# Fused block-sparse attention and ELU MLP: three of eight half-batches turned by VectorE and a DRAM scratch

## The chip, the cores and the metric

One core of a Trainium2 chip runs the whole program. The metric is device microseconds for one execution, the median of several. The core has TensorE (PE in the profile: matmuls; PEld: its weight loads), VectorE (DVE), ScalarE (ACT), GpSimd (POOL) and SyncE (SP). Each runs its own list of instructions in order, and waits on semaphores for the others. In this program SyncE does nothing but issue transfers, for 16 DMA engines.

## What is computed

Attention of 4 batches x 8 heads over 768 tokens with 64 dimensions. Each query takes, of the 24 chunks of 32 keys, the 6 with the largest upper bound of its scores. Then a two-layer MLP with ELU over the heads side by side:

```python
k_min, k_max = k_chunks.min(axis=3), k_chunks.max(axis=3)
ub = sum(maximum(q * k_min, q * k_max))           # per query and chunk, causal
sel = the 6 chunks with the largest ub
scores = where(sel & (i >= j), (q @ k.T) / 8, -1e9)
attn = softmax(scores) @ v                        # [4, 8, 768, 64]
x = attn.transpose(0, 2, 1, 3).reshape(3072, 512)
h = x @ w_in                                      # [3072, 2048]
g = where(h > 0, h, exp(min(h, 0)) - 1)
out = g @ w_out                                   # [3072, 512], float32
```

## The kernel before

Heads go in pairs, so that 2 x 64 dimensions fill the 128 partitions: pairs 0 to 3 are batch 0, pairs 4 to 7 batch 1, and so on. Queries go in halves of 384 (`HALF`), `hf` 0 or 1. For a pair and half, `pair_attend` makes the scores (L863) in pieces, takes their exponential on ScalarE (L890), and multiplies by v with a column of ones (L922, called PV below). VectorE takes the reciprocal of the row sums (L935) and multiplies (L938): the tile `on` holds 128 queries x 3 query tiles x 128 features. The MLP needs x with features on the partitions, so TensorE turns `on` in three 128x128 transposes into a PSUM bank (L947), and ScalarE copies the bank to SBUF as half of the tile `xT` (L950).

`mlp(b, hf)` multiplies by w_in in 16 blocks of 128 features of the hidden layer (L972, "up", four matmuls to a block, one for each pair), applies ELU with ScalarE (L982, L987) and VectorE (L990 to L1016), and multiplies by w_out (L1032, "down", in quarters of four matmuls), for three tiles of 128 tokens. ScalarE copies each tile to a result buffer `osb` (L1041), of which there are three, and SyncE stores it (L1046).

The order of work isn't left to a scheduler. The function is traced into a list of operations, each with its engine, what it reads and writes, and which buffers it takes and frees. `QUEUE` holds, for each engine, the numbers of these operations in the order in which the engine runs them; `Plan.order` only merges the five lists and hands out the numbered buffers, with a model of durations and of the DMA rings (`ALONE`, `SHARE`, `PAUSE`, `RAMP`). So PE's list mixes the MLP of one batch with the attention of the next. The number of buffers of each kind stands in `caps`:

```python
caps = {"S2": 2, "ps": 4, "H": 3, "O": 2, "T": 2, "M": 2, "MT": 2, ...,
        "pt": 10, "t": 3, "gT": 3, "osb": 3, "on": 3, "rc": 3, "xT": 8}
```

A buffer is taken again only when all that used it is over, a transfer out of it included. Loads of q, k and v and stores of results all stand in SyncE's one list; the eight weight transfers are issued by GpSimd. Keys and queries of batches 1 to 3 are loaded in pieces of 128 bytes (L592) and turned by VectorE in 32x32 blocks (L604, L622).

Of the kernel before, what the change touches and what calls it, by code (L numbers as in the profile page):

```python
# [14 lines left out]
BF16 = mybir.dt.bfloat16  # L15
# [58 lines left out]
    ],  # L74
    "POOL": [
# [10 lines left out]
    ],  # L86
    "ACT": [
# [20 lines left out]
    ],  # L108
# [5 lines left out]
    ],  # L114
# [43 lines left out]
class Plan:  # L158
# [71 lines left out]
    SHARE = {128: 1.0, 256: 0.35, 512: 0.3, 768: 0.3, 1024: 0.3, 2048: 0.5}  # L230
    HEAVY = 0.088
    RAMP = 240.0
    PAUSE = ((0.0, 2.28), (17.2, 17.8), (21.6, 22.4), (30.5, 31.3))
    LANDED = 0.75

    def served(self, rings, t, until):
# [877 lines left out]
```

## Time and profile before

| | |
|---|---|
| median of 3 runs | 273.88 us (272.23 to 274.41) |
| the profiled execution | 273.46 us, of which 271.8 us from its first to its last instruction |
| granted TensorE clock | 0.998 |
| packets moved by DMA | 112624, 29.79 MB; 101200 of them under 512 bytes |
| chain of work that ended last, PE's share | 78% |

A view of groups names the source line, the engine, the operation, what is written and read, and the count; then the busy time, the mean time of one, and the idle time of the engine just before, with what ended it. A view in order of time gives the start, the length, and in brackets the idle time before a row. In a view of stretches each engine has its busy time in that stretch, and then come the granted clock (1 is full), the mean busy share of the 16 DMA engines, and GB/s.

### The profile page before, as it was taken

To read this page: it belongs to the slowest core of one execution; us is meant where nothing else is said; L and a number is where in the kernel's file an instruction comes from. 1 tells how busy PE (TensorE), PEld (TensorE's weight loads), DVE (VectorE), ACT (ScalarE), POOL (GpSimd) and SP (SyncE) were. 2 spreads that over 40 slices of the span, in tenths; PEclk is the share of its full clock that TensorE was granted. 3 is DMA by queue.
4 is the path that set the end of the run, shared out by engine and by line. 5 is a ranking of instruction groups with operands and counts; after the bars stand their busy time and mean duration, and the time that the engine had idled before them with its cause. 6 is when DMAs were issued, how large, how long until landed. Compare 5 with 4: busy or idle time off the path is not lost.

```text
span 271.8 us, 6603 instructions
## 1 busy us (share of the span) xinstructions
PE 258.6 (95%) x2456; PEld 160.0 (59%) x2456; DVE 206.8 (76%) x532; ACT 200.0 (74%) x375; POOL 118.3 (44%) x209
## 2 busy tenths in 40 slices
PE   3898899999999899999999999999999999999995
PEld 3787566655565455655565556665666655555544
DVE  5698979899999979889998867786666875137530
ACT  3899999846996589989899478977898744243512
POOL 3577783155876696870874055544330000000000
PEclk9999999999999999999999999999999999999999
DMA  7997999999999995999931010000210101110113
GB/s 218 266 211 124 205 216 214 164 176 151 148 203 130 192 169 115 139 156 201 240 103 41 1 58 22 0 2 3 76 41 1 41 2 39 39 41 0 65 53 116
DMA packets 112624, 29.79 MB, mean 110 GB/s; under 512 B 101200, under 2 KB 109648, under 8 KB 112592
## 3 DMA queue, kind: packets, MB, share of 16 engines
q1 hardware_dynamic: 107280, 24.39, 48.5%
q0 software_dynamic: 4224, 4.19, 9.3%
q10 hardware_dynamic: 1088, 0.79, 0.9%
q8 instruction: 19, 0.31, 0.5%
q14 instruction: 13, 0.11, 0.1%
HBM read 27.26 MB, written 6.29 MB: 123 GB/s over the span
## 4 chain that ended last, share of the span: by engine, by line
PE 78%; ACT 7%; DVE 6%; DMA 6%; issue 1%; SPq 1%; POOL 0%; DVEq 0%; ACTq 0%; POOLq 0%
PE psH L972 20%; PE psM L1032 20%; PE psS L863 10%; PE psS L972 8%; PE psMT L1032 8%; PE psO L922 6%; ACT pt L890 3%; DMA w_in_sb<-in_moe_w_in_dram 3%; PE psS L771 2%; ACT lhs L695 2%; PE psT L947 2%; DMA out_dram<-osb 1%; PE psMT L685 1%; DMA gT<-in_k_dram 1%; PE psH L685 1%
## 5 line engine op out<-in xcount | busy, mean ns | idle before, releaser
L890 ACT ACTIVATE pt<-psS 128x768 bf16<-128x768 f32 (+1 forms) x120 | 89.8, 781 | 11.3 <-PE psS L863 6.7
L972 PE MATMUL psH<-xT,w_in_sb 128*128 128x384 bf16 x384 | 73.7, 326 | 0.5 <-DMA w_in_sb<-in_moe_w_in_dram 0.4
L1032 PE MATMUL psM<-w_out_sb,gT 128*128 128x512 bf16 x288 | 72.1, 379 | 0.0
L972 PEld LDWEIGHTS <-w_in_sb 128*128 128x128 bf16 x512 | 47.7, 97 | 33.1 <-issue 1.3
L863 PE MATMUL psS<-rhs,lhs 88*128 88x384 bf16 (+4 forms) x304 | 54.6, 283 | 2.8 <-ACT pt L890 2.8
L1032 PEld LDWEIGHTS <-gT 128*128 128x128 bf16 x400 | 37.3, 97 | 33.0 <-DVE gT L1016 0.5
L982 ACT ACTIVATE f<-psH 128x384 f32<-128x384 f32 x96 | 47.0, 506 | 7.0 <-PE psH L972 6.1
L909 POOL TENSOR_SCALAR_AFFINE_SELECT pt<-pt 128x512 bf16<-128x512 bf16 (+1 forms) x48 | 24.7, 522 | 61.6 <-ACT pt L890 58.1
L1011 DVE SCALAR_TENSOR_TENSOR t<-f,psH 128x384 bf16<-128x384 f32 x56 | 30.1, 547 | 12.9 <-ACT f L982 12.4
L863 PEld LDWEIGHTS <-lhs 88*128 88x128 bf16 x304 | 27.4, 98 | 17.8 <-issue 3.0
L737 POOL CAST rhs<-f 64x768 bf16<-64x768 f32 (+1 forms) x40 | 27.7, 698 | 20.4 <-DVE f L622 8.6
L821 POOL COPY rhs<-selt 24x576 bf16<-24x576 bf16 (+2 forms) x40 | 22.7, 566 | 24.2 <-DVE selt L810 22.5
L922 PEld LDWEIGHTS <-pt 128*128 128x128 bf16 x672 | 28.3, 98 | 7.4 <-issue 1.0
L1016 DVE SCALAR_TENSOR_TENSOR gT<-psH,t 128x384 bf16<-128x384 f32 x56 | 30.5, 551 | 1.1
L922 PE MATMUL psO<-vext,pt 128*128 128x65 bf16 x672 | 31.1, 194 | 0.1
L950 ACT ACTIVATE xT<-psT 128x384 bf16<-128x384 bf16 x32 | 15.6, 497 | 11.9 <-PE psT L947 11.9
L972 PE MATMUL psS<-xT,w_in_sb 128*128 128x384 bf16 x128 | 22.9, 326 | 0.0
L982 ACT ACTIVATE f<-psS 128x768 f32<-128x768 f32 x16 | 13.0, 811 | 13.5 <-PE psS L972 13.5
L990 DVE SCALAR_TENSOR_TENSOR gT<-f,psH 128x384 bf16<-128x384 f32 x40 | 21.3, 541 | 2.0 <-ACT psH L987 1.3
L1032 PE MATMUL psMT<-w_out_sb,gT 128*128 128x512 bf16 (+1 forms) x112 | 22.6, 349 | 0.0
L737 POOL CAST lhs<-f 64x768 bf16<-64x768 f32 x24 | 19.7, 823 | 6.4 <-DVE f L604 5.5
L987 ACT ACTIVATE psH<-psH 128x384 f32<-128x384 f32 x40 | 20.2, 512 | 0.0
(55 smaller groups left out, 278.9 us busy)
## 6 DMA issues: line engine op xcount, KB each, us to landing
out_dram<-osb SPq DMA_DIRECT2D x23, 256.0 KB, 2.2
f<-in_k_dram SPq DMA_DIRECT2D x48, 96.0 KB, 3.9
f<-in_q_dram SPq DMA_DIRECT2D x48, 96.0 KB, 3.8
f<-in_v_dram SPq DMA_DIRECT2D x24, 192.0 KB, 3.9
w_in_sb<-in_moe_w_in_dram POOLq DMA_DIRECT2D x4, 512.0 KB, 9.2
w_out_sb<-in_moe_w_out_dram POOLq DMA_DIRECT2D x4, 512.0 KB, 14.7
gT<-in_k_dram SPq DMA_DIRECT2D x8, 192.0 KB, 4.3
gT<-in_v_dram SPq DMA_DIRECT2D x12, 128.0 KB, 4.2
```

The source lines that it names most:

```text
L737: nc.gpsimd.tensor_copy(out=o, in_=i)
L821: eng.tensor_copy(out=dst.rearrange("c h (i two x) -> c h i two x", two=2, x=32)[:, :, :, odd, :], in_=tiles[st][r0:r0 + NCH, c0:c0 + n].r ...
L863: nc.tensor.matmul(p_s[:, hd, pc:pc + w], lhsT=tiles[pt_["kb"]][0:64 + NCH, hd, 128 * kb:128 * kb + 128], rhs=tiles[pt_["qb"]][0:64 + NCH, ...
L890: lambda bs=bs, pt=pt, wtot=wtot, lo=lo, at=at: nc.scalar.activation(out=tiles[pt][:, :, lo:lo + wtot], in_=tiles[bs[0]][:, :, at:at + wto ...
L909: nc.gpsimd.affine_select(out=a, in_=a, compare_op=AOT.is_ge, fill=0.0, base=0, pattern=pat, channel_multiplier=-1)
L922: nc.tensor.matmul(po[:, hd, qi, :], lhsT=tiles[pt][:, hd, off:off + 128], rhs=tiles[pt_["vx"]][:, 6 * hd + kb, :], start=(kb == 0), stop= ...
L972: nc.tensor.matmul(ph, lhsT=w_in_sb[:, kk, f0:f0 + 128], rhs=tiles[XT[4 * b + kk]][:, c0:c0 + HALF], start=(kk == 0), stop=(kk == NKK - 1))
L982: lambda e=e, view=view: nc.scalar.activation(out=halves(e)[:, 0:step], in_=view(), func=AF.Exp),
L990: lambda e=e, view=view, fc=fc, gt=gt: nc.vector.scalar_tensor_tensor(out=tiles[gt][:, fc:fc + step, :], in0=halves(e)[:, 0:step], scalar= ...
L1011: lambda e=e, t=t, view=view: nc.vector.scalar_tensor_tensor(out=tiles[t][:, 0:step], in0=halves(e)[:, 0:step], scalar=1.0, in1=view(), op ...
L1016: lambda t=t, view=view, fc=fc, gt=gt: nc.vector.scalar_tensor_tensor(out=tiles[gt][:, fc:fc + step, :], in0=view(), scalar=0.0, in1=tiles ...
L1032: nc.tensor.matmul(pm, lhsT=tiles[gt][:, fc, 128 * tt:128 * tt + 128], rhs=w_out_sb[:, fc, x0:x1], start=(fc == 0), stop=(fc == NFC - 1))
```

## The change

For the halves in `TURN`, both of batch 2 and the first of batch 3, `on` no longer goes to TensorE. VectorE transposes its 32x32 blocks into a second tile of the same kind, `xb`; four transfers write that to a scratch in DRAM so that the blocks land where the whole transpose has them, in pieces of 96 elements; and one transfer loads the scratch as half of `xT`. The columns of `xT` are then in another order of tokens: column 96i + 32t + r of the half holds its token 128t + 32i + r. So the stores of these halves go out in two parts each, to the rows to which they belong. The other halves are done as before. In `pair_attend`:

```diff
+            if (u // 4, hf) in TURN:
+                xb, = new("on")
+                there = dram.tile([P, HALF], BF16, name=f"xd{u}_{hf}")
+                def flat(h):
+                    return tiles[h].rearrange("p q h d -> p (q h d)")
+                def blocks():
+                    nc.vector.transpose(out=flat(xb).rearrange("p (j t x) -> p t j x", j=4, x=32),
+                                        in_=flat(on).rearrange("p (t j x) -> p t j x", j=4, x=32))
+                def put():
+                    for i in range(4):
+                        nc.sync.dma_start(out=there[:, 96 * i:96 * i + 96].rearrange("(j a) y -> a j y", j=4),
+                                          in_=flat(xb)[32 * i:32 * i + 32].rearrange("a (j y) -> a j y", j=4))
+                add("DVE", dve(HALF), pr, blocks, reads=[on], writes=[xb], alloc=[xb], free=[on])
+                fetch(4, 128, 192, pr, put, [("put", u, hf)], more=[xb], free=[xb])
+                fetch(1, 128, 768, pr,
+                      lambda: nc.sync.dma_start(out=tiles[xt_h][:, HALF * hf:HALF * hf + HALF], in_=there[:, :]),
+                      [(xt_h, hf)], more=[("put", u, hf)], alloc=[] if hf else [xt_h])
+                return
             bx = bank("T")
```

And in `mlp`, where a tile of results is stored:

```diff
+                    if (b, hf) in TURN:
+                        def put(osb=osb, row=b * S + HALF * hf, tt=tt, x0=x0, x1=x1):
+                            o4 = out[row:row + HALF, x0:x1].rearrange("(t i r) y -> i t r y", i=4, r=32)
+                            for p0, i, t0, n in (((0, 0, 0, 3), (96, 1, 0, 1)), ((0, 1, 1, 2), (64, 2, 0, 2)),
+                                                 ((0, 2, 2, 1), (32, 3, 0, 3)))[tt]:
+                                nc.sync.dma_start(out=o4[i, t0:t0 + n],
+                                                  in_=tiles[osb][p0:p0 + 32 * n, 0:x1 - x0])
+                        add("SP", 1.066, pr, put, reads=[osb], free=[osb], move=(0, 1.08, 0.533, 2, 64, 4 * w))
+                        continue
```

The five lists of `QUEUE` are other lists throughout, for operations of all batches. In the planner's model some numbers change (among them eight more entries in `PAUSE`, `RAMP` as a delay, a share of 0.75 to 0.25 for two unlike transfers); these issue no instruction of their own. The free of `xb` is entered in the model at the issue of the puts; the program itself waits for their landing.

More of the change, by code (lines that the diff above doesn't have):

```diff
@@ L227, in clocked @@
         return dur if warm else dur + dur
-    ALONE = {128: 0.0138, 256: 0.0188, 512: 0.036, 768: 0.0368, 1024: 0.055, 2048: 0.085}
-    SHARE = {128: 1.0, 256: 0.35, 512: 0.3, 768: 0.3, 1024: 0.3, 2048: 0.5}
+    ALONE = {128: 0.0138, 192: 0.0166, 256: 0.0188, 512: 0.036, 768: 0.0376, 1024: 0.055, 2048: 0.085}
+    SHARE = {128: 1.0, 192: 0.6, 256: 0.35, 512: 0.3, 768: 0.3, 1024: 0.3, 2048: 0.5}
     HEAVY = 0.088
     RAMP = 240.0
-    PAUSE = ((0.0, 2.28), (17.2, 17.8), (21.6, 22.4), (30.5, 31.3))
+    PAUSE = ((0.0, 2.28), (17.2, 18.0), (21.8, 22.6), (30.5, 31.3), (53.0, 54.0), (61.0, 62.0), (67.0, 68.2), (80.6, 81.6), (85.4, 86.2), (98.0, 99.0), (108.0, 109.0), (117.0, 118.0))
     LANDED = 0.75
@@ L257, in served @@
             if heavy and heavy[0][4]:
-                heavy[0][1] += self.RAMP
+                heavy[0][0] = t + self.RAMP * self.HEAVY / 16
                 heavy[0][4] = 0
+                continue
             rate = {}
@@ L269, in served @@
                     rate[e] = 16 / cyc
+            if not heavy and len(heads) == 2:
+                (e0, h0), (e1, h1) = heads
+                c0, c1 = self.ALONE[h0[2]], self.ALONE[h1[2]]
+                if max(c0, c1) > 1.5 * min(c0, c1):
+                    rate[e0] = 16 / c0 * (0.75 if c0 < c1 else 0.25)
+                    rate[e1] = 16 / c1 * (0.75 if c1 < c0 else 0.25)
             first = min(heads, key=lambda x: x[1][1] / rate[x[0]])
@@ L409 @@
     work = ctx.enter_context(tc.tile_pool(name="work", bufs=1))
+    dram = ctx.enter_context(tc.tile_pool(name="dram", bufs=1, space=bass.MemoryType.DRAM))
     psum = ctx.enter_context(tc.tile_pool(name="psum", bufs=1, space=bass.MemoryType.PSUM))
@@ L567, in weights @@
             move=(2, 1.75, 0.0, 1, 512, 1024))
-        add("DMA", 0.0, -20.0, lambda: None, reads=[("asked", i)], writes=[name], lat=plan.LANDED)
+        add("DMA", 0.0, -20.0, lambda: None, reads=[("asked", i)], writes=[name], lat=plan.LANDED + (0.8 if i else 0.3))
     def fetch(starts, packets, size, pr, f, writes, eng="SP", more=(), **kw):
@@ L574, in fetch @@
         add(eng, 0.533 * starts, pr, f, reads=more, writes=[w] + writes, lat=0.0,
-            move=(0 if eng == "SP" else 1, 1.08 if eng == "SP" else 1.3, 0.533, starts, packets, size), **kw)
+            move=(0 if eng == "SP" else 1, 1.08 if eng == "SP" else 1.75, 0.533, starts, packets, size), **kw)
         add("DMA", 0.0, pr, lambda: None, reads=[w], writes=writes, lat=plan.LANDED)
+    TURN = ((2, 0), (2, 1), (3, 0),)
     PAIR = {}
@@ L1044, in mlp @@
                     row = b * S + HALF * hf + 128 * tt
+                    if (b, hf) in TURN:
[6 more added lines that the diff above has]
+                        add("SP", 1.066, pr, put, reads=[osb], free=[osb], move=(0, 1.08, 0.533, 2, 64, 4 * w))
+                        continue
                     add("SP", 0.533, pr,
```

170 rows, old and new, of the table QUEUE are left out of this document.

## The prediction

> **What bounds the kernel now.** I read the busy times first, then the same in stretches, then the one stretch that differs.
>
> ```profile
> span 271.8 us, 6603 instructions
> PE 258.6 (95%) x2456; PEld 160.0 (59%) x2456; DVE 206.8 (76%) x532; ACT 200.0 (74%) x375; POOL 118.3 (44%) x209
> ```
> ```profile
> core 0: us, PE busy (x) PEld busy (x) DVE busy (x) ACT busy (x) POOL busy (x), PEclk, DMA share, GB/s
> 0.00:24.00 24.00, 17.81 (x243) 15.60 (x244) 17.17 (x66) 18.43 (x44) 13.85 (x43) 1.00 0.99 221
> 24.00:48.00 24.00, 22.45 (x275) 15.58 (x273) 21.93 (x67) 22.86 (x45) 16.51 (x27) 1.00 1.32 194
> 48.00:88.00 40.00, 39.51 (x398) 23.04 (x396) 38.63 (x106) 30.30 (x56) 23.61 (x37) 1.00 1.05 162
> 88.00:96.00 8.00, 6.42 (x63) 3.81 (x62) 8.00 (x13) 4.93 (x8) 5.46 (x8) 1.00 1.31 183
> 96.00:136.00 40.00, 40.00 (x387) 23.77 (x386) 36.25 (x97) 36.65 (x73) 26.96 (x45) 1.00 0.98 171
> 136.00:212.00 76.00, 76.00 (x730) 46.46 (x729) 55.63 (x143) 63.33 (x118) 31.31 (x52) 1.00 0.09 31
> 212.00:264.00 52.00, 52.00 (x337) 28.40 (x336) 29.22 (x46) 22.09 (x35) 0.64 (x1) 1.00 0.10 37
> 264.00:272.00 8.00, 4.44 (x37) 3.34 (x35) 0.00 (x0) 1.37 (x3) 0.00 (x0) 0.91 0.27 98
> ```
>
> PE is never idle from 96 to 264 us, at full granted clock. So the end is set by three things: PE's work, PE's idle time before 96 (6.19 in the first 24 us, 1.55 in the next, 0.49, then 1.58 between 88 and 96), and the last stores. An edit that takes work from PE after 96 gains it in full, and a wait that it puts there is paid in full. The DMA engines are full until about 136 us (share near 1), and nearly idle afterwards.
>
> The 1.58 us have one cause, seen in four views: SyncE's queue, ScalarE, PE, and the stores of results.
>
> ```profile
> 84.84 4.94 SPq L592 DMA_DIRECT2D f<-in_k_dram  x8
> 89.82 0.61 SPq L1046 DMA_DIRECT2D out_dram<-osb  x1
> ```
> ```profile
> 89.82 3.55 DMA out_dram<-osb
> ```
> ```profile
> 93.39 0.60 ACT L1041 ACTIVATE osb<-psM 128x512 f32<-128x512 f32 x1 [1.74 <-DMA out_dram<-osb]
> 94.74 0.49 PE L863 MATMUL psS<-rhs,lhs 88*128 88x384 bf16 x2 [1.36 <-ACT pt L890]
> 95.44 0.48 PE L863 MATMUL psS<-rhs,lhs 88*128 88x384 bf16 x2 [0.22 <-ACT pt L890]
> ```
> ```profile
> L1046 SPq DMA_DIRECT2D out_dram<-osb x25: 332/357/1698, 89.8 to 268.9; - x25
> L1041 ACT ACTIVATE osb<-psM x18: 591/597/705, 60.7 to 241.6; 128x512 f32<-128x512 f32 x18
> ```
>
> The first result was in its buffer at 60.7 us, but its store was issued only at 89.8, behind loads in SyncE's list. There are three result buffers; the fourth copy waited 1.74 us for that store to land, the exponentials queued behind it on ScalarE, and PE lost 1.36 + 0.22 = 1.58.
>
> **The change, part by part.** The prices:
>
> ```profile
> L950 ACT ACTIVATE xT<-psT 128x384 bf16<-128x384 bf16 x32 | 15.6, 497 | 11.9 <-PE psT L947 11.9
> L947 PE MATMUL psT<-ident_b,on 128*128 128x128 bf16 x96 | 10.3, 219 | 0.9 <-DVE on L938 0.8
> L938 DVE TENSOR_TENSOR on<-psO,rc 128x384 bf16<-128x384 f32 x32 | 17.5, 554 | 0.7
> L935 DVE RECIPROCAL rc<-psO 128x6 f32<-128x6 f32 x32 | 5.9, 189 | 15.9 <-PE psO L922 15.6
> L810 DVE STREAM_TRANSPOSE selt<-selv 128x384 bf16<-128x384 bf16 x2 | 1.2, 578 | 0.0
> ```
> ```profile
> 142.26 0.33 PE L947 MATMUL psT<-ident_b,on 128*128 128x128 bf16 x3
> 142.43 1.02 PE L1032 MATMUL psM<-w_out_sb,gT 128*128 128x512 bf16 x4
> 143.30 0.49 PE L863 MATMUL psS<-rhs,lhs 88*128 88x384 bf16 x2
> 143.62 0.81 PE L972 MATMUL psH<-xT,w_in_sb 128*128 128x384 bf16 x4
> 144.28 0.49 PE L863 MATMUL psS<-rhs,lhs 88*128 88x384 bf16 x2
> 144.60 0.54 PE L922 MATMUL psO<-vext,pt 128*128 128x65 bf16 x12
> 144.98 2.11 PE L972 MATMUL psH<-xT,w_in_sb 128*128 128x384 bf16 x12
> ...
> 177.41 1.12 PE L922 MATMUL psO<-vext,pt 128*128 128x65 bf16 x30
> 178.37 0.81 PE L972 MATMUL psH<-xT,w_in_sb 128*128 128x384 bf16 x4
> ```
> ```profile
> 128.25 1.06 SPq L634 DMA_DIRECT2D f<-in_v_dram  x2
> ```
> ```profile
> out_dram<-osb SPq DMA_DIRECT2D x16, 256.0 KB, 2.1
> out_dram<-osb SPq DMA_DIRECT2D x2, 128.0 KB, 1.7
> ```
> ```profile
> f<-in_q_dram SPq DMA_DIRECT2D x48, 96.0 KB, 3.8
> ```
> Matmuls overlap, so what a group costs PE is the distance to the next start: transposes of one half 142.43 - 142.26 = 0.17, a quarter of a down row-block 0.87, two score matmuls 0.32, one up block 0.66, PV of a first half 0.38, PV of a second half 178.37 - 177.41 = 0.96. The DMA rows are the last 136 us (stores), and the whole run (loads).
>
> *Removed from PE.* Three halves of four pairs each lose their transposes: 12 x 0.17 = 2.0 us, all after 96, where PE is the bound: -2.0. The TensorE price has a rule of the Trainium skill against it: VectorE: DVE Perf Modes, section "The three transpose paths", puts one 128x128 transpose on TensorE at 390 ns, which would make the 36 of them worth 14.0 us. No run here shows that: three start and are passed in 0.17.
>
> *Removed from ScalarE*: 12 x 0.497 = 6.0 us, which PE's full stretches hide: nothing.
>
> *Added to VectorE*: a block transpose per half, priced by the only one of this size and type, 0.578: 12 x 0.578 = 6.9 us. By their place in the new order all but the first come after 136 us, in the stretch where VectorE is busy 55.63 of 76 us. Nothing, as long as no matmul waits for the very next VectorE result.
>
> *Added to SyncE*: 12 x 5 transfers, and 9 more stores (nine tiles in two parts each), 69 x 0.53 = 37 us of issuing (1.06 for two), nearly all of it after 136 us, where only result stores are left. The bytes of the stores stay, 2 KB to a row. The last four stores are those of before: the tail stays.
>
> *The way round.* Before, a half was in place 0.17 + 0.50 us after the division. Now: reciprocal 0.19, division 0.55, block transpose 0.58 (together 1.32), four puts issued 0.53 apart (the fourth starts 1.6 later), their landing L, the load back, L again. With 1.7 and 2.1 for stores on idle DMA engines, and puts of 24 KB, I take L = 2.0; the bounds are 1.7 below and, above, 3.8, the loads in 128-byte pieces on full engines. PE stalls if its order holds less work than this between the last PV and the first up block. I add up the new order of instructions at the three places:
> - batch 2, first half, pair 11: six down quarters (5.2), four pairs of scores (1.3) and a PV of 0.96 stand between: 7.5. Path: 1.32 + 1.6 + 2L = 6.9. Covered, up to L = 2.3.
> - batch 2, second half, pair 8: 8.9 us of such work. Covered.
> - batch 3, first half: here the buffers bind. The normalized tiles have three buffers, a half now takes two, and in the new order pair 15's block transpose waits for pair 14's puts, whose buffer it overwrites. From pair 14's last PV: 1.32 + (1.6 + L) + 0.58 + (1.6 + L) + L = 5.1 + 3L = 11.1. PE has three down quarters (2.6), six pairs of scores (1.9), seven up blocks (4.6), pair 15's PV 0.38 and 0.17: 9.7. A stall of 1.4; with L = 1.7, 0.5; with 3.8, 6.8. Behind the waiting VectorE stand the ELU steps of seven up blocks, so PE may wait for their PSUM banks first; that is the same time, not a second one.
>
> *The lists.* What changes most for PE ahead of 96 is the store. SyncE's new list has 74 transfers ahead of the first one, the old list 92; at the pace of the row above (8 loads in 4.94 us) that is 11 us sooner, about 79 instead of 89.8, and landed 3.55 us later, at 82. The fourth copy comes after as much PE work as before, so not much ahead of 93.39. That wait goes: -1.6. Next late could be the fifth copy, which needs the second store: behind 99 transfers, so issued near 94 and landed near 98, while PE has 9.6 us of work between the fourth copy and the fifth. Covered by some 4 us; I take nothing for it. The order of the first 48 us is little changed: nothing, with 1 us either way.
>
> Sum: -2.0 - 1.6 + 1.4 = -2.2. The profiled execution took 273.46 us (span 271.8), so 271.3; the median of the runs shown, 273.88, stands 0.4 higher, so about 271.6.
>
> **Rivals.**
> *All of it is hidden.* If L is 1.7 and the store waits vanish, only 0.5 of the way round is left, and if the start gains 0.3 of the 1 us that I left open: -2.0 - 1.6 + 0.5 - 0.3 = -3.4, or 270.5. For it: the loads after 137 us are gone. Against: every semaphore handover that I left out lengthens the path.
>
> *The store wait comes back.* The puts stand in SyncE's list ahead of stores: those of pair 9's second half wait for VectorE, and two stores and a load stand behind them. With three buffers a later copy waits, as the one at 93.39 did. Then the 1.6 is not gained: -2.0 + 1.4 = -0.6, 273.3.
>
> *Slower: the landing decides.* The scratch is written in pieces of 192 bytes and read back at once. If L is as under load, both round trips show. The first place stalls by 2L - 4.6, the last by 5.1 + 3L - 9.7: together more than 3.6 from L = 2.6 on. With 3.2 it is 1.8 + 5.0, less 3.6: +3.2, 277.1; with 3.8, 3.0 + 6.8 - 3.6 = +6.2. For it: the loads' 3.8; against: the stores' 2.1 after 136. DMA: Bandwidth & Descriptors of the Trainium skill, section "Specifications", says that transfers under 512 bytes are read, modified and written, and speaks for this rival; no run here shows such writes to DRAM.
>
> *The transposes were worth more.* If each group costs PE its recorded 3 x 0.219, twelve are worth 7.9, not 2.0: -7.9 - 1.6 + 1.4 = -8.1, or 265.8. That is the skill's price in kind; the starts in the timeline speak against it.
>
> **How the numbers follow.** The forecast has 0.46, with a range of its own from 270.5 to 273.0; all hidden 0.19; the store wait back 0.2; the slow landing 0.14; the dear transposes 0.01. The range from 269.6 to 275.0 takes in the hidden case and the returned wait, and about a third of the slow landing. One per cent, about what a measurement of this kernel can tell from none (the runs shown lie 0.8% apart), is 271.1 and 276.6. Faster: the hidden case, the dear transposes, and four tenths of the forecast, whose middle lies 0.5 above the bound: 0.38. Slower: most of the slow landing and a little of what I have not seen: 0.13. The rest, 0.49, is within 1%.
>
> **What would show it.** PE's count falls by 36 matmuls and by no more than about 2 us of time; no ScalarE copy waits for a store near 90 us; PE shows one idle piece just ahead of batch 3's first up block, released by the load from the scratch, of 0.5 to 2 us, and VectorE one ahead of pair 15's block transpose, released by a put. The median from issue to landing of the puts is the number that makes or breaks it: above 2.6 us I am wrong on the sign; if the store wait shows again, by the 1.6.

## The result, and the profile after

The changed kernel took 280.22 us (median of five runs, 278.40 to 280.96), the kernel before beside it 273.68 (272.23 to 274.41): a ratio of 1.0234, with a 95% interval of 1.0201 to 1.0267. It is slower by 6.5 us, where 271.6 was forecast. The profiled execution has a span of 278.6 us against 271.8, so 6.8 us are to be found.

The head of the page of the changed kernel, with the busy times of the engines and the row of granted clocks in 40 slices:

```profile
span 278.6 us, 6640 instructions
...
PE 259.7 (93%) x2396; PEld 160.0 (57%) x2420; DVE 212.2 (76%) x544; ACT 195.1 (70%) x363; POOL 117.9 (42%) x209
...
PEclk9999999999999999999999999999997799999999
```

PE's busy time has grown by 1.1 us with fewer matmuls. (36 fewer would leave 2420, as the weight loads show; 24 matmul records are missing from this trace.) The clock row has two slices at seven tenths, where that of the kernel before is nines throughout. The view of stretches, with the same columns and stretches as in the prediction but for the last, which ends later:

```profile
0.00:24.00 24.00, 19.02 (x254) 16.75 (x255) 17.64 (x73) 19.18 (x46) 14.83 (x44) 1.00 1.04 225
24.00:48.00 24.00, 22.17 (x281) 15.40 (x278) 21.79 (x63) 21.70 (x41) 15.82 (x27) 1.00 1.27 183
48.00:88.00 40.00, 39.35 (x390) 23.17 (x392) 38.53 (x105) 30.64 (x56) 22.84 (x35) 1.00 1.08 168
88.00:96.00 8.00, 7.94 (x69) 4.68 (x67) 7.97 (x13) 6.38 (x10) 6.99 (x11) 1.00 1.04 128
96.00:136.00 40.00, 39.67 (x368) 23.21 (x371) 37.32 (x99) 35.81 (x71) 26.58 (x44) 1.00 0.93 166
136.00:212.00 76.00, 70.94 (x680) 43.12 (x685) 56.94 (x148) 56.31 (x102) 30.24 (x51) 1.00 0.26 65
212.00:264.00 52.00, 50.03 (x310) 27.35 (x316) 29.02 (x45) 21.68 (x34) 0.64 (x1) 0.93 0.15 33
264.00:281.00 17.00, 10.61 (x67) 6.34 (x65) 3.03 (x4) 3.39 (x6) 0.00 (x0) 0.91 0.23 78
```

PE's idle time ahead of 96 us is each stretch less its busy time: 4.98 + 1.83 + 0.65 + 0.06 = 7.5, before 9.8. That is 2.3 won. From 96 to 264 there was none before; now it is 0.33 + 5.06 + 1.97 = 7.4. Both hold short pieces that stand right before a group of down matmuls with a missing record: 0.27 us in all ahead of 96 and 0.97 behind it. They are work that the trace does not show. Without them 2.6 us are won ahead of 96 and 6.4 lost behind it. Nearly all of the 6.4 is one wait. The timeline of the changed kernel, first SyncE, then VectorE, then PE (start, length, what, and in brackets the idle time before the row):

```profile
199.12 1.26 SPq L1080 DMA_DIRECT2D out_dram<-osb  x2
200.49 0.48 SPq L969 DMA_DIRECT2D xT<-xd  x1
201.02 1.49 SPq L1080 DMA_DIRECT2D out_dram<-osb  x2
202.63 11.75 SPq L964 DMA_DIRECT2D xd<-on  x8
```
```profile
204.14 0.56 DVE L947 TENSOR_TENSOR on<-psO,rc 128x384 bf16<-128x384 f32 x1
212.04 0.58 DVE L959 STREAM_TRANSPOSE on<-on 128x384 bf16<-128x384 bf16 x1 [7.34 <-DMA xd<-on]
212.54 0.51 DVE L1041 SCALAR_TENSOR_TENSOR t<-f,psH 128x384 bf16<-128x384 f32 x1
213.09 0.56 DVE L1046 SCALAR_TENSOR_TENSOR gT<-psH,t 128x384 bf16<-128x384 f32 x1
```
```profile
206.95 0.49 PE L872 MATMUL psS<-rhs,lhs 88*128 88x384 bf16 x2
213.71 1.46 PE L1002 MATMUL psH<-xT,w_in_sb 128*128 128x384 bf16 x4 [6.27 <-DVE gT L1046]
214.96 0.85 PE L872 MATMUL psS<-rhs,lhs 88*128 88x384 bf16 x2
```

Four part stores (L1080) are issued ahead of pair 14's four puts (L964, at 202.63; the group of eight includes pair 15's four, near its end). VectorE divides pair 15's half by 204.70, and then waits 7.34 us with the block transpose, whose buffer pair 14's puts are still reading. Behind it stand the ELU steps, and PE waits 6.27 us for the first of them. One of pair 14's puts, issued at 205.83, is timed there: 6.0 us. The list of issues gives, for the whole run and then for 205 to 225 us, count, size, and the median from issue to landing of the transfers that can be timed (6 of the 48, and that one of the 7):

```profile
xd<-on SPq DMA_DIRECT2D x48, 24.0 KB, 1.6
```
```profile
xd<-on SPq DMA_DIRECT2D x7, 24.0 KB, 6.0
```

So the ordinary put lands in 1.6 us, and the late one stands behind the part stores.

The wait costs more than itself. PE's first four matmuls afterwards take 1.46 us, against 0.81 in the prediction's rows. The view of stretches just there:

```profile
213.70:215.00 1.30, 1.29 (x5) 0.62 (x6) 1.27 (x3) 0.00 (x0) 0.00 (x0) 0.50 0.25 49
...
218.00:219.00 1.00, 1.00 (x5) 0.45 (x3) 0.56 (x1) 0.72 (x1) 0.00 (x0) 0.50 0.28 70
219.00:220.00 1.00, 1.00 (x7) 0.52 (x5) 0.00 (x0) 0.00 (x0) 0.00 (x0) 0.78 0.22 27
```

The granted clock is 0.50 from 213.7 until about 219.4 (0.78 over the last microsecond means half speed for 0.44 of it): 5.7 us at half speed lose 2.9. PE's work therefore fell by 0.5 only: its busy time grew by 1.11, the missing records add 1.24, and 2.87 of it is the half clock.

The tail is longer too. PE's last matmul ended 3.3 us before the end, and now 4.0, with a ScalarE copy that waits for a result buffer:

```profile
274.59 0.38 ACT L1071 ACTIVATE osb<-psMT 128x256 f32<-128x256 f32 x1 [2.79 <-DMA out_dram<-osb]
```

The sum: -2.6 (idle ahead of 96), -0.5 (PE's work), +6.4 (idle behind 96), +2.9 (half clock), +0.7 (tail), together +6.9, for the 6.8 between the spans.

### The profile page after: what moved, and what is told of

Read it like the earlier page. It is cut to its first block, busy times and chain, and to the rows that moved or that the text cites. A ratio compares the mean times of both kernels' runs of the same rounds, so it can differ in the third digit from the quotient of the medians.

```text
span 278.6 us, 6640 instructions
## 1 busy us (share of the span) xinstructions
PE 259.7 (93%) x2396; PEld 160.0 (57%) x2420; DVE 212.2 (76%) x544; ACT 195.1 (70%) x363; POOL 117.9 (42%) x209
## 4 chain that ended last, share of the span: by engine, by line
PE 80%; DMA 7%; ACT 6%; DVE 3%; issue 1%; SPq 1%; POOL 0%; ACTq 0%; DVEq 0%; POOLq 0%
PE psM L1062 21%; PE psH L1002 21%; PE psS L872 11%; PE psS L1002 7%; PE psO L931 7%; PE psMT L1062 6%; DMA w_in_sb<-in_moe_w_in_dram 3%; PE psS L780 3%; ACT lhs L704 2%; DMA xd<-on 2%; ACT pt L899 1%; PE psH L694 1%; DMA out_dram<-osb 1%; DMA gT<-in_k_dram 1%; PE psT L977 1%
## 5 line engine op out<-in xcount | busy, mean ns | idle before, releaser
L899 ACT ACTIVATE pt<-psS 128x768 bf16<-128x768 f32 (+2 forms) x120 | 89.7, 780 | 12.5 <-PE psS L872 8.4
L1002 PE MATMUL psH<-xT,w_in_sb 128*128 128x384 bf16 x384 | 76.6, 333 | 7.7 <-DVE gT L1046 6.3
L1002 PEld LDWEIGHTS <-w_in_sb 128*128 128x128 bf16 x512 | 48.4, 99 | 42.7 <-DVE gT L1046 7.1
L1062 PE MATMUL psM<-w_out_sb,gT 128*128 128x512 bf16 x267 | 68.2, 379 | 1.2 <-issue 0.2
L1012 ACT ACTIVATE f<-psH 128x384 f32<-128x384 f32 x96 | 47.4, 505 | 17.7 <-PE psH L1002 14.9
L872 PE MATMUL psS<-rhs,lhs 88*128 88x384 bf16 (+4 forms) x304 | 55.5, 286 | 0.4 <-ACT pt L899 0.3
L872 PEld LDWEIGHTS <-lhs 88*128 88x128 bf16 x304 | 28.5, 98 | 16.3 <-issue 1.6
L931 PEld LDWEIGHTS <-pt 128*128 128x128 bf16 x672 | 27.2, 98 | 6.3 <-issue 0.7
L931 PE MATMUL psO<-vext,pt 128*128 128x65 bf16 x672 | 29.3, 193 | 0.1
L1030 DVE TENSOR_SCALAR t<-f 128x768 bf16<-128x768 f32 x16 | 8.9, 559 | 17.8 <-ACT f L1012 17.8
L1017 ACT ACTIVATE psH<-psH 128x384 f32<-128x384 f32 x40 | 21.0, 524 | 0.0
```

Source lines behind the costliest of these rows:

```text
L872: nc.tensor.matmul(p_s[:, hd, pc:pc + w], lhsT=tiles[pt_["kb"]][0:64 + NCH, hd, 128 * kb:128 * kb + 128], rhs=tiles[pt_["qb"]][0:64 + NCH, ...
L899: lambda bs=bs, pt=pt, wtot=wtot, lo=lo, at=at: nc.scalar.activation(out=tiles[pt][:, :, lo:lo + wtot], in_=tiles[bs[0]][:, :, at:at + wto ...
L931: nc.tensor.matmul(po[:, hd, qi, :], lhsT=tiles[pt][:, hd, off:off + 128], rhs=tiles[pt_["vx"]][:, 6 * hd + kb, :], start=(kb == 0), stop= ...
L1002: nc.tensor.matmul(ph, lhsT=w_in_sb[:, kk, f0:f0 + 128], rhs=tiles[XT[4 * b + kk]][:, c0:c0 + HALF], start=(kk == 0), stop=(kk == NKK - 1))
L1012: lambda e=e, view=view: nc.scalar.activation(out=halves(e)[:, 0:step], in_=view(), func=AF.Exp),
L1062: nc.tensor.matmul(pm, lhsT=tiles[gt][:, fc, 128 * tt:128 * tt + 128], rhs=w_out_sb[:, fc, x0:x1], start=(fc == 0), stop=(fc == NFC - 1))
```

## The experiments

My theory (A) was that the part stores delay the puts queued behind them; its rival, that of the prediction, that the puts' own small writes are slow. In the trace's records of packets (start, size, time taken; first and last are starts), the 256 rows of 2048 bytes of the four part stores stand in one place and those of two whole stores of the first experiment in another:

```
                     rows   first us   last us   DMA engines' time us
changed kernel        256     200.40    210.78      28.4
whole stores (e1)     256     198.22    200.30      22.0
```

28.4 us of engine time in 10.4 us is 2.7 engines at work; 22.0 in 2.1 is 10.5. Why it would be so few I did not know yet.

**Whole stores.** e1_whole_rows takes the part stores out:

```diff
-                    if (b, hf) in TURN:
-                        def put(osb=osb, row=b * S + HALF * hf, tt=tt, x0=x0, x1=x1):
...
-                        add("SP", 1.066, pr, put, reads=[osb], free=[osb], move=(0, 1.08, 0.533, 2, 64, 4 * w))
-                        continue
```

> The changed kernel, but the tiles of results of the three halves are stored whole, 128 rows in one transfer, in the order of the columns (so the rows of these halves lie in another order in the output). Theory A (the part stores): in the changed kernel the stores in parts of 32 and 96 rows keep only two or three DMA engines busy, about 9 us for four of them; pair 14's puts stand behind them and one lands 6.0 us after its issue, VectorE waits 7.3 us, PE 6.3, and then PE runs about 6 us at half clock, which costs 3.0. With whole stores these puts land in 1.6 to 2 us like the others, VectorE waits 1 to 2 us, PE at most 1.5, the clock stays: 280.2 - 5 - 3 = 272, give or take 1. Theory B (the three buffers or the way through DRAM are what costs; the stores are innocent): stays at 279 to 281.

It took 271.3, a ratio of 0.9933 (0.9905 to 0.9960). The timeline of e1_whole_rows at the same place:

```profile
200.85 5.96 SPq L964 DMA_DIRECT2D xd<-on  x8
...
204.48 0.58 DVE L959 STREAM_TRANSPOSE on<-on 128x384 bf16<-128x384 bf16 x1 [1.56 <-DMA xd<-on]
...
206.15 0.82 PE L1002 MATMUL psH<-xT,w_in_sb 128*128 128x384 bf16 x4 [0.49 <-DVE gT L1046]
```

VectorE's wait fell from 7.34 to 1.56 us, PE's from 6.27 to 0.49 (0.85 with a second piece of 0.36), and the clock stays full. The same puts, in the same 192-byte pieces, are fast when the stores beside them are whole.

**A fourth buffer.** e2_on4 keeps the part stores and gives the normalized tiles four buffers, so that the block transpose need not wait:

```diff
-            "osb": 3, "on": 3, "rc": 3, "xT": 8}
+            "osb": 3, "on": 4, "rc": 3, "xT": 8}
-    econ = const.tile([P, S], BF16, name="econ")
+    econ = work.tile([P, S], BF16, name="econ", tag="xT7")
```

> The changed kernel with four buffers for the normalized tiles instead of three (a start-up constant moved into another buffer to make room), stores in parts as in the change. Theory A: VectorE no longer waits before pair 15's block transpose, but pair 14's and 15's puts still land late behind the part stores, near 212 us, and the loads back 2 us later; PE does its remaining 4.5 us of up blocks first and then waits about 3 us at batch 3's first up block instead of 6.3: about 276 (275 to 278). Theory B with the buffers as the cause: no wait of VectorE, PE waits under 1 us: 271 to 272.

277.06, a ratio of 1.0136 (1.0084 to 1.0187). The timeline of e2_on4, VectorE and then PE:

```profile
207.91 0.58 DVE L959 STREAM_TRANSPOSE on<-on 128x384 bf16<-128x384 bf16 x1
...
217.13 4.40 PE L1002 MATMUL psS<-xT,w_in_sb 128*128 128x384 bf16 x15 [2.83 <-DMA xT<-xd]
```

The wait for the buffer is gone, and what is late next is the load of batch 3's first half from the scratch: PE waits 2.83 us for it. The slow puts are only met later. (In this profile, the slowest of the four runs, PE also lost 3.29 us near 52 us, which the other kernels do not show there: VectorE waits 3.83 us for a load of q, and the clock halves for 3.4 us behind it. Why that load was late stays open. The two quickest runs took 275.9.)

**The part stores alone.** e6_before_split is the kernel before with the part stores of the changed kernel and nothing else of it:

```diff
+    TURN = ((2, 0), (2, 1), (3, 0),)
...
+                    if (b, hf) in TURN:
+                        def put(osb=osb, row=b * S + HALF * hf, tt=tt, x0=x0, x1=x1):
...
+                        continue
```

> The kernel before, all as it was but the result tiles of both halves of batch 2 and the first of batch 3, which go out in the change's two parts each (rows of these halves in another order in the output). This prices the part stores by themselves. Theory A: the parts of 32 and 96 rows land clearly later than the 2.0 to 2.2 us of whole stores, 64 KB parts in 2.5 us or more although they are a quarter of a tile, 192 KB parts near 3.5 to 4; nothing waits for them but the three result buffers, so the time is 273.7 to 275. Theory B: they land in 1.7 to 2.2 us, time unchanged within 0.3%.

276.35, a ratio of 1.0131 (1.0094 to 1.0168): 3.2 us slower, more than I expected, and with no put in the program. The time goes at the end. The timelines of the kernel before and of e6_before_split there:

```profile
265.61 3.66 SPq L1046 DMA_DIRECT2D out_dram<-osb  x4
267.17 0.38 ACT L1041 ACTIVATE osb<-psMT 128x256 f32<-128x256 f32 x1 [1.58 <-PE psMT L1032]
```
```profile
264.98 0.60 ACT L1042 ACTIVATE osb<-psMT 128x512 f32<-128x512 f32 x1 [1.82 <-DMA out_dram<-osb]
265.60 5.69 SPq L1056 DMA_DIRECT2D out_dram<-osb  x4
269.57 0.38 ACT L1042 ACTIVATE osb<-psMT 128x256 f32<-128x256 f32 x1 [3.99 <-DMA out_dram<-osb]
```

A copy that waited for PE now waits 3.99 us for a part store to give back its buffer. But of the smallest parts, of 32 rows, the two that can be timed landed in 1.6 and 1.9 us, where I had expected 2.5 or more of each part. So not all parts are slow in themselves, and that pointed to their shape: a part is written as n x 32 x 512, with n of 3, 2 or 1. The packets of two parts with n = 2 (128 rows, 228.28 to 234.51 us, 12.7 us of engine time) keep two engines busy, and these two transfers end with 4 semaphore writes in all, where a put makes 16.

**The same bytes in parts of 32 rows.** e7_32rows cuts each part into its n pieces, so that the outermost length of each is 32:

```diff
-                                nc.sync.dma_start(out=o4[i, t0:t0 + n],
-                                                  in_=tiles[osb][p0:p0 + 32 * n, 0:x1 - x0])
+                                for j in range(n):
+                                    nc.sync.dma_start(out=o4[i, t0 + j],
+                                                      in_=tiles[osb][p0 + 32 * j:p0 + 32 * j + 32, 0:x1 - x0])
```

> The changed kernel, with each part store of 2 x 32 or 3 x 32 rows cut into transfers of 32 rows each: four to a tile, the same rows and bytes. Theory A1 (a transfer is spread over as many engines as its outermost length, so 2 or 3 engines for these parts, and 16 for a store with 32 or 128 rows outermost): the stores end in time, pair 14's puts land in 1.6 to 2 us, PE idles at most 1.5 us near 206, 271.5 to 273. Theory A2 (what counts is the number of partitions, or that the tile goes out in small parts): four parts are no better than two, 278 or more.

273.17, a ratio of 0.9987 (0.9962 to 1.0012). Twice as many part stores, and 7 us faster than the changed kernel, though just above the 271.5 to 273 that I expected, and 1.9 above e1_whole_rows. PE's waits in e7_32rows:

```profile
208.55 0.82 PE L1002 MATMUL psH<-xT,w_in_sb 128*128 128x384 bf16 x4 [1.57 <-DVE gT L1046]
...
210.06 0.81 PE L1002 MATMUL psH<-xT,w_in_sb 128*128 128x384 bf16 x4 [0.36 <-DVE gT L1046]
```

**One store, two shapes.** Cutting also changes how many transfers there are. So the last pair keeps the whole stores of e1_whole_rows, one for a tile, and changes only the order in which the rows are named: for the halves in TURN, with a = 2 in e9_outer2 and a = 16 in e10_outer16. Against the changed kernel:

```diff
                     if (b, hf) in TURN:
-                        def put(osb=osb, row=b * S + HALF * hf, tt=tt, x0=x0, x1=x1):
...
+                            lambda osb=osb, row=row, x0=x0, x1=x1: nc.sync.dma_start(
+                                out=out[row:row + 128, x0:x1].rearrange("(r a) y -> a r y", a=2),
+                                in_=tiles[osb][:, 0:x1 - x0]),
...
```

> The kernel of e1_whole_rows, where each result tile of the three halves leaves in one store of 128 rows of 2 KB; here the same store, with the same bytes and packets, is written with an outermost length of 2 on the DRAM side (even rows, then odd rows, so rows of these halves lie in another order still). Theory A (the outermost length sets how many DMA engines carry a transfer): two stores ahead of pair 14's puts hold two engines for 64 x 84 ns = 5.4 us each, the puts land after 6 to 9 us, VectorE's block transpose of pair 15 waits 6 to 10 us, PE 5 to 9, and the half clock follows: 278 to 283 us. Rival B (it is the number of transfers, or of SyncE's issues, that delays the puts): as e1_whole_rows, 271.3 within 1.

> The same with an outermost length of 16 (rows of these halves in a third order): the rows go to scattered addresses as in the run before, but theory A expects 16 engines and so the time of e1_whole_rows, 271.3 within 1, with PE waiting about 0.9 us ahead of batch 3's first up block. Rival C (scattered rows of a store are slow in themselves): as the run before, 278 or more.

With an outermost length of 2 it took 282.76, a ratio of 1.0365 (1.0320 to 1.0410); with 16, 271.32, a ratio of 0.9943 (0.9918 to 0.9968). The lists of issues from 200 to 213 us, e9_outer2 (where one of the four can be timed) and then e10_outer16, and PE's rows and the packets of the whole run in the same order:

```profile
xd<-on SPq DMA_DIRECT2D x4, 24.0 KB, 8.4
```
```profile
xd<-on SPq DMA_DIRECT2D x8, 24.0 KB, 1.6
```
```profile
214.64 1.46 PE L1002 MATMUL psH<-xT,w_in_sb 128*128 128x384 bf16 x4 [8.07 <-DVE gT L1046]
```
```profile
207.12 0.82 PE L1002 MATMUL psH<-xT,w_in_sb 128*128 128x384 bf16 x4 [0.90 <-DVE gT L1046]
```
```profile
DMA packets 121138, 32.15 MB, mean 114 GB/s; under 512 B 108178, under 2 KB 118162, under 8 KB 121106
```
```profile
DMA packets 121264, 32.15 MB, mean 119 GB/s; under 512 B 108304, under 2 KB 118288, under 8 KB 121232
```

The same count of transfers, bytes and rows of 2 KB, and one number in an access pattern is worth 11.4 us. The 126 packets fewer in e9_outer2 are small ones, 14 for each of the nine stores: two semaphore writes to a store in place of sixteen. The packets of two stores took 12.1 us (199.54 to 211.68; 24.2 us of engine time, so two engines at work) with an outermost length of 2, and 2.9 us (199.21 to 202.12; 31.5, so 10.8 at work) with 16. Neither scattered rows nor the number of issues explain that: theory A stands, and rivals B and C fall.

The Trainium skill states this rule: DMA: Bandwidth & Descriptors, section "Why a DMA increments its semaphore by 16 and not by 1", says that a transfer is split over the largest number of engines, at most 16, that divides the slowest length above one on both of its sides, and that on a queue like that of SyncE these are the lowest-numbered ones. The runs agree with the first part: parts of 96 rows by 3 or 64 by 2 leave 3 or 2 engines, 32 rows leave 16. The records do not name the engine of a packet, and so not its number. But that the narrow stores crowd onto the same engines, and hold up a put that uses all 16, can be read from the times of the semaphore writes at the end of each transfer (each narrow store has one more, about 1 us after its issue):

```
                               semaphore writes, us
e9, store issued at 198.26     206.31, 206.75
e9, store issued at 199.53     211.69, 212.10
e9, put issued at 201.77       14 of them 205.03 to 205.77; 211.94, 212.32
e10, put issued at 201.40      16 of them 202.63 to 203.92
```

The second store ends 5.4 us behind the first, the time of its 64 packets of 84 ns on an engine, so both used the same two. Fourteen shares of the put have landed by 205.77, and the last two land right behind the second store: its other two engines were those of the stores.

**The lists without the turn.** Two kernels keep the new lists of the changed kernel and let TensorE turn all halves, with its transposes put 1.5 us of PE's work behind the last PV in e5_lists_only and 3.5 us in e8_lists_late:

```diff
-    TURN = ((2, 0), (2, 1), (3, 0),)
+    TURN = ()
```

> The new lists without the new way: all halves turned by TensorE and copied by ScalarE as before, the transposes put into the new PE list some 1.5 us of work behind the last PV of their half, the copies at the matching place of ScalarE's list; no scratch, no part stores. This prices the lists alone. From the two profiles PE's idle time ahead of 96 us is 9.8 before and 7.5 with the new lists: 273.7 - 2.3 = 271.4 (270.5 to 272.5), if the lists are as good as the old ones after 96 us. If the new lists are also a loss behind 96 us (written for another set of operations), 273 or more.

> As e5 (the new lists, all halves turned by TensorE), but each transpose stands 3.5 us of PE work behind its last PV instead of 1.5. In e5's profile PE waited some 3.4 us in all for the division ahead of transposes. If e5's loss is the place that I chose, it falls by 2 to 3 us, to 273.5 to 274.5, and the new lists are worth little by themselves. If it is the lists: stays at 276.

276.44 (ratio 1.0128, 1.0097 to 1.0160) and 276.53 (1.0117, 1.0096 to 1.0138). The first misses the 271.4 that I expected of the lists alone; the second stays at 276, as expected if it is the lists and not the place. The rows of 136 to 212 us, e5_lists_only and then e8_lists_late, and the busy times of e5_lists_only:

```profile
136.00:212.00 76.00, 73.25 (x714) 44.26 (x713) 53.33 (x140) 58.17 (x109) 29.99 (x50) 1.00 0.12 36
```
```profile
136.00:212.00 76.00, 73.19 (x695) 44.26 (x702) 53.32 (x140) 58.88 (x110) 28.80 (x49) 1.00 0.12 36
```
```profile
PE 261.1 (95%) x2456; PEld 160.7 (58%) x2456; DVE 206.4 (75%) x532; ACT 199.9 (73%) x375; POOL 117.9 (43%) x209
```

The idle time ahead of 96 is won here too (6.7 and 6.5 us against 9.8), but PE loses 2.8 in this stretch in pieces that no single wait explains (some of them missing records in e8_lists_late). And in e5_lists_only PE is busy for 261.1 us with the same 2456 matmuls that take 258.6 before: the new order costs 2.5 us of PE's busy time by itself. Why is not shown. The lists were made for halves that need neither PE nor ScalarE to be turned; with the old steps put back, ScalarE copies wait longer for transposes (L985, 14.9 us in e5_lists_only; 11.9 before). That 2 us more between a PV and its transposes make no difference doesn't rule out a better place. What the lists alone are worth stays open.

**What beats both.** e3_up_order keeps whole stores and leaves no row displaced: the up matmuls read the half of xT in the order of tokens, in pieces of 64 bytes, so g and the result come out in the old order. e4_up_order_on4 is that with the fourth buffer of e2_on4.

```diff
-                            nc.tensor.matmul(ph, lhsT=w_in_sb[:, kk, f0:f0 + 128],
-                                             rhs=tiles[XT[4 * b + kk]][:, c0:c0 + HALF],
+                            rhs = tiles[XT[4 * b + kk]][:, c0:c0 + HALF]
+                            if (b, hf) in TURN:
+                                rhs = rhs.rearrange("p (i t r) -> p t i r", i=4, r=32)
+                            nc.tensor.matmul(ph.rearrange("p (t i r) -> p t i r", i=4, r=32) if (b, hf) in TURN else ph,
+                                             lhsT=w_in_sb[:, kk, f0:f0 + 128], rhs=rhs,
...
-                    if (b, hf) in TURN:
-                        def put(osb=osb, row=b * S + HALF * hf, tt=tt, x0=x0, x1=x1):
...
-                        continue
```

> The changed kernel with whole stores as in e1, and the tokens put right elsewhere: the up matmuls of these halves read xT in the order of tokens (pieces of 32 columns, 64 bytes), so the output has its rows where they belong. Theory A (the part stores are the loss): as e1, 271.3, give or take 0.8, PE's idle time near 206 us about 0.85. Rival: the moving operand in 64-byte pieces streams slower; 192 of these matmuls at 0.163 us are 31 us, so 10% slower is 3 us: 274 or more, and the up blocks of these halves take more than 0.65 us.

> As e3, with four buffers for the normalized tiles. If the three buffers cost what e1's profile shows (VectorE 1.56 us ahead of pair 15's block transpose, PE 0.85 us behind it), PE has no wait there: 0.8 us less than e3, 270.5. If the buffers no longer matter once the puts land in time: the same as e3 within 0.3%.

270.96, a ratio of 0.9909 (0.9884 to 0.9933), and 269.71, a ratio of 0.9868 (0.9848 to 0.9888). The timeline of e4_up_order_on4, VectorE and PE:

```profile
203.54 0.58 DVE L959 STREAM_TRANSPOSE on<-on 128x384 bf16<-128x384 bf16 x1
...
206.09 0.81 PE L1005 MATMUL psH<-xT,w_in_sb 128*128 128x384 bf16 x4
```

Neither engine waits there any more, and four matmuls on 64-byte pieces take the 0.81 of those on whole rows. e3_up_order came as theory A had it; the fourth buffer gave 1.25 us, where 0.8 was expected.

## Why the prediction was wrong, step by step

*The step that failed* and gave the sign is in the part on SyncE: "9 more stores (nine tiles in two parts each)" were priced by their issue alone, and "The bytes of the stores stay, 2 KB to a row." The bytes stay, but the rows go through 2 or 3 DMA engines instead of 16. I read the sizes of the pieces in the new access pattern and not its outermost length. By e9_outer2 and e10_outer16 that alone is worth 11.4 us; by e1_whole_rows against the changed kernel, 8.9 (280.22 - 271.3, from two sets of runs).

*L = 2.0.* The puts by themselves are as I took them: 1.6 us as a median over all 48 of e1_whole_rows, and 1.5 to 2.7 for those of pair 14, where PE waits 0.85 and the sum had 1.4. In the changed kernel the put timed at that place took 6.0, for the reason above.

*The place* was right for VectorE: pair 15's block transpose waits for pair 14's puts. PE does not show it just ahead of batch 3's first up block, released by the load from the scratch, but four up blocks earlier, released by the ELU steps behind VectorE; the prediction allowed for that in its working, not in its signs. With the fourth buffer the wait goes from VectorE, and then PE does wait for that load.

*The half clock* was in no sum: I priced a stall at its own length. After 6.27 us it cost 2.9 more.

*The tail* "stays", I wrote. The last four stores did, but the copy ahead of them needs a buffer that a part store holds: 0.7 us in the changed kernel, and most of the 3.2 in e6_before_split, where PE's last matmul ends 6.2 us before the end.

*PE's work* was the second term to fail: -2.0 forecast, about -0.5 found. Two kernels with whole stores, whose traces have all 2420 matmul records, agree. e1_whole_rows and then e10_outer16, against 258.6 before:

```profile
PE 258.4 (96%) x2420; PEld 159.5 (59%) x2420; DVE 211.7 (79%) x544; ACT 194.9 (73%) x363; POOL 117.8 (44%) x209
```
```profile
PE 258.0 (96%) x2420; PEld 158.7 (59%) x2420; DVE 212.3 (79%) x544; ACT 195.1 (72%) x363; POOL 117.7 (44%) x209
```

Counted as in the prediction, from start to next start, the transposes take 5.6 us before and 4.1 in e1_whole_rows, 1.5 less. The new order makes PE's other groups dearer. In *The lists* I priced the store wait and gave the order no price in PE's own time; e5_lists_only, with the old steps put back, has it at 2.5.

*What came as forecast.* The first store is issued at 78.1 us (79 forecast). The store wait between 88 and 96 us is gone: 7.94 busy of 8 (1.6 forecast, 1.5 measured), and the idle time of the first 24 us, left open by 1 us, fell by 1.2. The block transposes take 0.578 as priced, and hide. The dear transposes did not show: no run gains anything near 8 us. With whole stores the change gives -1.8 (271.3 against 273.12), close to the -2.2 of the sum, but by luck. The profiled execution of e10_outer16, 2.5 us shorter than that of before, is made of -3.4 (idle ahead of 96), -0.6 (PE's work), +1.3 (idle behind 96) and +0.2 (tail): PE idles less at the start than I gave the lists, and works more.

*The rival that had the sign.* "The landing decides" had the chain and the formula, and put the cost of L = 3.8 at a 6.8 us stall at the last place, near the 6.27 seen, which is luck. Its cause, writes of 192 bytes, is not what happened: the same writes land in 1.6 us in e10_outer16 and e1_whole_rows. The read, modify and write of pieces under 512 bytes, which the Trainium skill (DMA: Bandwidth & Descriptors, section "Specifications") sets against such puts, shows no price here: these 1.6 us stand beside 1.7 for stores of 128 KB in e1_whole_rows.

## What to carry to other kernels

Read the outermost length of both sides of each transfer that an edit adds or reshapes, not only its bytes and the size of its pieces: 2 or 3 there make a store several times longer, and what is issued behind it waits too. A short transfer behind a narrow one is as late as the narrow one, so look for what is queued after it and who waits for that. And price a PE stall of some microseconds with the half clock behind it, 1.6 to 2.9 us here.

## What the runs showed that I had not expected

A DMA's shape, not its size, set its speed: 256 rows of 2 KB took 12.1 us with an outermost length of 2, and 2.9 us with 16.

The granted clock fell to 0.50 at PE's waits of 2.83 us (e2_on4), 6.27 (the changed kernel) and 8.07 (e9_outer2), and not at that of 1.57 (e7_32rows). The stretches of e2_on4:

```profile
217.00:218.00 1.00, 0.72 (x2) 0.21 (x2) 0.00 (x0) 0.00 (x0) 0.00 (x0) 0.50 0.73 212
...
220.00:221.00 1.00, 1.00 (x7) 0.54 (x5) 0.10 (x1) 0.81 (x1) 0.00 (x0) 0.84 0.19 66
```

PE worked at half speed for 3.2 us there (from 217.13 to about 220.3), and for 5.7 in the changed kernel. The Trainium skill, TensorE: Matmul & The Clock Gate, section "Part 1: The HAM clock gate (the "warmup" mystery)", has the clock halve after an idle window of about 3.4 us and come back after a busy one, and says that the window runs free of what the kernel does. The traces agree with the two levels and with the grid. From fall to return the clock's records show 3.41 us in e2_on4 (from 216.91), 6.83 in the changed kernel (from 212.62) and 10.24 in e9_outer2 (from 209.31), which is once, twice and three times 3.413. But PE need not be idle for a whole window. In the 3.41 us ahead of these falls it was idle for 2.61 (e2_on4), all (the changed kernel) and 2.73 (e9_outer2). The window before that in the changed kernel, with 1.77 of idle, brought no fall. So a stall of 2.83 us can be enough, by where it lies.
